# Attention and MLP in one kernel: an even pace for weight rounding, a later broadcast of inverted sums, and a direct inversion for the third pair

## The chip, the cores and the metric

The kernel runs on one core of one Trainium2 chip. The core's engines each work through their own instruction list in order: PE (TensorE, matrix products), DVE (VectorE), ACT (ScalarE), POOL (GpSimd) and SP (SyncE, which here only issues DMAs). The metric is device microseconds of one execution, as the median over several executions. "PEld" in the profile is the loading of PE's weights.

## The reference

Routed attention over 4 batches x 8 heads, 768 positions, head width 64, followed by an MLP without bias. A query attends only to keys that fall to the same of 16 centroids.

```python
q_assign = np.argmax(np.einsum('bhsd,hcd->bhsc', q_n, c_n), axis=-1)
k_assign = np.argmax(np.einsum('bhsd,hcd->bhsc', k_n, c_n), axis=-1)
mask = q_assign[:, :, :, None] == k_assign[:, :, None, :]
scores = np.where(mask, scale * np.matmul(q, k.transpose(0, 1, 3, 2)), -1000000000.0)
attn = np.exp(scores - np.max(scores, axis=-1, keepdims=True))
attn = attn / (np.sum(attn, axis=-1, keepdims=True) + 1e-09)
x = np.matmul(attn, v)      # regrouped to (3072, 512)
h = x @ w_in                # 512 x 2048
out = (h - np.tanh(h)) @ w_out
```

The two weight matrices are float64 in memory; everything else is float32.

## The kernel before

**Pairs and steps.** Two heads make a pair `n`; there are 16 pairs, four to a batch (`HP` = 4). A pair's 768 queries are handled in two halves of `TB` = 384, and the keys of a half in three steps of two 128-row tiles (`NS` = 3). The list `steps` (L850) gives 96 steps: 0 to 11 are half 0 of pairs 0 to 3, 12 to 23 their half 1, and from step 24 each pair takes six steps. The loop at L976 writes one step after another, and the order in which it writes is the order on each engine.

**One step.** `begin` (L411) computes the scores of the *following* step on PE (L419; in half 0 of pairs 1 to 3 a masking product on `hot`, L430, is added) and their exponential on ACT (L441). `value` (L466) multiplies the weights of this step with the values (L473) and, in half 0 of batch 0, also with a column of ones (L482), which gives the softmax sums. In all other halves `select` (L443) applies the mask on DVE (L451) and POOL adds up the weights (L460, L464). Two score buffers and three general PSUM buffers (`ps_f`) are shared by everything; `av` has one buffer, so `value` of a new half waits until `take` (L489, ACT) has emptied it into `xT`.

**Softmax sums.** When a half is complete (its third step, T), `total` (L494) puts the sums into a tile `den` (128 x 384, two buffers), each head's row repeated over 64 partitions. To divide, the kernel does not invert all of `den`. It writes one row per head to DRAM (`list`, L511), reads them back spread over 128 partitions (`each`, L522, step T+1), inverts 128 x 6 elements (`invert`, L528, T+2), writes them to DRAM (`back`, L530), broadcasts them back over `den` (two DMAs, L532, also T+2), and multiplies `xT` with them (`scale`, L538, T+3). The fourth pair of a batch (`last`, L517) is different: `divide` (L540) inverts `den` in place in three pieces of 128 columns (L543), multiplies (L546), and POOL keeps account of the sums and inverses (L507, L547). The list is written by this line, `i` being the step after T:

```python
for i, stage in enumerate((total, compact, invert, scale)):
```

**Weight rounding.** `w_in` and `w_out` come as 32 pieces of 512 KB in float64 words. A piece goes through: `fetch` (L185, a DMA issued by POOL into one of three `raw` buffers), `rest_of` (L195, one ACT pass, L140, into one of two `rest` buffers), `round_piece` (L200, three DVE passes, L145, L149, L152), which frees the `raw` buffer and fetches piece `at + 3`. Two pieces are rounded ahead of the loop. In the loop `paces` (L973) gives the number for each step: none in steps 0 to 2, one in steps 3 and 4, two from step 5 to step 18. On ACT, `rest_of` stands between the exponentials of the following step and `take`; on DVE, `round_piece` stands last in the step, behind `invert` and `scale`.

**What is woven in.** From step 12, batch 0's MLP products (`up` L557 with L565, then `project` L575 with L581) fill steps 12 to 47; from step 48 a Strassen form of the same for batches 1 to 3 (L755, L803), whose factors are read back from DRAM (`stream`, L681). The pieces of a pair's preparation (`turn`, `similar`, `route`, `publish`, `spread_both`, `one_hot`) are placed by `ready`. For pair 3 they are: `route` in step 4, `publish` (`q_codes`, L370) and `spread_both` (`hot`, L386) in step 5, `one_hot` (L394, L398) in step 7; step 9's scores, written in step 8, are the first to use that `hot`.

Of the kernel before, what the change touches and what calls it, by code (L numbers as in the profile page):

```python
# [30 lines left out]
F32 = mybir.dt.float32  # L31
# [7 lines left out]
P = 128  # L39
# [18 lines left out]
def kernel(  # L58
# [14 lines left out]
    B, H, S, D = q.shape  # L73
# [4 lines left out]
    HP = H // 2  # L78
# [3 lines left out]
    TB = S // 2  # L82
# [9 lines left out]
    const = ctx.enter_context(tc.tile_pool(name="const", bufs=1))  # L92
    dram = ctx.enter_context(tc.tile_pool(name="dram", bufs=6, space=DRAM))
# [7 lines left out]
    wholes = const.tile([P, TB], F32, name="wholes")  # L101
    smallest = const.tile([P, 2 * len_pieces], F32, name="smallest")
    largest = const.tile([P, 4 * (HP - 1)], F32, name="largest")
    each = const.tile([P, 2 * B * (HP - 1), 2 * TB // P], F32, name="each")
    flag = const.tile([1, 1], I32, name="flag")

    out_r = out.rearrange("(b p j) m -> b j p m", p=P, j=NCH)
# [30 lines left out]
    def low_words(dst, raw, rest):  # L138
        lo, _, rest = shaped(dst, raw, rest)
        nc.scalar.activation(out=rest, in_=lo, func=ACT.Copy, scale=2.0**-29)  # L140

    def high_words(dst, raw, rest):
        _, hi, rest = shaped(dst, raw, rest)
        bits = dst.bitcast(U32)
        nc.vector.tensor_scalar(  # L145
            out=bits, in0=hi, scalar1=3, scalar2=0x3FFFFFF8,
            op0=ALU.logical_shift_left, op1=ALU.bitwise_and,
        )
        nc.vector.scalar_tensor_tensor(  # L149
            out=bits, in0=hi, scalar=0xC0000000, in1=bits, op0=ALU.bitwise_and, op1=ALU.bitwise_or  # L150
        )
        nc.vector.tensor_tensor(out=bits, in0=bits, in1=rest, op=ALU.add)  # L152

    def fast():
# [30 lines left out]
        def fetch(at: int):  # L185
            if at >= len(PIECES):
                return
            dst, src = PIECES[at]
            if words == 1:
                nc.gpsimd.dma_start(dst, src)  # L190
                return
            raws[at] = rawp.tile([P, 2 * FQ * P], U32, name="raw")
            nc.gpsimd.dma_start(raws[at], src)

        def rest_of(at: int):  # L195
            if words == 2 and at < len(PIECES):
                rests[at] = restp.tile([P, FQ * P], U32, name="rest", tag="rest")
                low_words(PIECES[at][0], raws[at], rests[at])

        def round_piece(at: int):  # L200
            if words == 2:
                high_words(PIECES[at][0], raws.pop(at), rests.pop(at))
            fetch(at + AHEAD)
# [72 lines left out]
        pairs = [(b, p) for b in range(B) for p in range(HP)]  # L276
# [217 lines left out]
        def total(n: int, half: int):  # L494

            s = sums.pop((n, half))
            ps = s
            if not summed(n, half):
                ps = ps_f.tile([P, TB], F32, name="den", tag="f")
                for h in range(2):  # L500
                    nc.tensor.matmul(  # L501
                        ps[h * D : h * D + D], lhsT=ones, rhs=s[:, h], start=True, stop=True
                    )
            t = dens[n, half] = sump.tile([P, TB], F32, name="den")
            nc.scalar.activation(out=t, in_=ps, func=ACT.Copy, bias=EPS)
            if last(n):
                nc.gpsimd.tensor_tensor(out=wholes, in0=wholes, in1=t, op=ALU.add)  # L507
                return
            lists[n, half] = dram.tile([2, TB], F32, name="list")
            for h in range(2):  # L510
                nc.sync.dma_start(lists[n, half][h : h + 1], t[h * D : h * D + 1])  # L511
# [2 lines left out]

        lists, spots = {}, {}

        def last(n: int):  # L517
            return pairs[n][1] == HP - 1

        def compact(n: int, half: int):  # L520
            spots[n, half] = each[:, len(spots)]
# [4 lines left out]
        def invert(n: int, half: int):  # L526
            t = spots[n, half]
            nc.vector.reciprocal(out=t, in_=t)  # L528
            back = dram.tile([2, TB], F32, name="back")
            nc.sync.dma_start(back.rearrange("h n -> (h n)").rearrange("(p i) -> p i", p=P), t)  # L530
            for h in range(2):
                nc.sync.dma_start(  # L532
                    dens[n, half][h * D : h * D + D], back[h : h + 1].to_broadcast([D, TB])
                )
# [313 lines left out]
        NS = NCH // 2  # L848
        HALF = HP * NS
# [120 lines left out]
            fills[2 * (b + 1) * HALF] = (lambda b=b: strassen_items(b), 2 * HALF)  # L970


        paces = {3: 1, 4: 1}  # L973
        late, divides, makers, later = [], [], [], {}
        fill, whole, spent, since, over = [], 0.0, 0.0, 0, 1
        for at, (n, half, s) in enumerate(steps):  # L976
            b, p = pairs[n]
            following = steps[at + 1] if at + 1 < len(steps) else None
            after = steps[at + 2] if at + 2 < len(steps) else None
            if at == 4 * HALF:  # L980
                open_late()
            if at == 4 * HALF - 9:
                open_stream()
            if at in fills:
                fill, over = fills[at][0](), fills[at][1]
                whole, spent, since = sum(it[0] for it in fill), 0.0, at
            if at == 2 * HALF:
                makers = [it for i in range(2) for it in up_maker(i)]
                makers += [it for i in range(2) for it in down_maker(i)]
            now = []  # L990
            part = (at - since + 1) / over
            while fill and (spent + fill[0][0] / 2 <= whole * part or part == 1):
                now.append(fill.pop(0))
                spent += now[-1][0]
            stages = ready.get(at, {})
            if 1 in stages:
                stages[1]()
            if after and after[2] == 0 and not masked(*after[:2]):
                spread(*after[:2])
            if following and at >= NS - 1:  # L1000
                begin(following)
            share = paces.get(at, 0 if at < NS else 2)
            todays, rounding = rounding[:share], rounding[share:]
            for piece in todays:
                rest_of(piece)
            value(n, half, s)
            if s == NS - 1:
                take(n, half)
                if last(n):
                    divides = [lambda n=n, half=half, i=i: divide(n, half, i) for i in range(HCH)]  # L1010
                else:
                    for i, stage in enumerate((total, compact, invert, scale)):
                        later.setdefault(at + i, []).append(
                            lambda stage=stage, n=n, half=half: stage(n, half)
                        )

                if p == HP - 1 and (half == 1 or b == 0):
                    total(n, half)
                    late += divides
                    divides = []  # L1020
                if half == 1:
                    load(n + (HP if n < 2 else 2), (2,) if n < 2 or n >= HP else ())

            todo = []
            if following:
                todo += [lambda i=i: select(*following[:2], 2 * following[2] + i) for i in range(2)]
            todo += [stages[i] for i in (5, 3, 4, 2) if i in stages]
            todo += late + later.pop(at, [])
            late = []
            if divides:  # L1030
                todo.append(lambda n=n, half=half: total(n, half))
                late, divides = divides, []
            todo += [lambda piece=piece: round_piece(piece) for piece in todays]

            light = [i for i in range(at, 4 * HALF - 2) if i % 3 and i % 6 != 1]
            if makers and at in light:
                share = -(-len(makers) // len(light))
                todo += makers[:share]
                del makers[:share]
            if "raw" in late_pools:  # L1040
                todo += [check_done, check_done, check_on, check_on]
            slots = max(sum(it[1] for it in now), 1)
            place = iter(range(slots))
            turned_at = max(slots - 1 - now[-1][1], 0) if now else 0

            def between():
                i = next(place)
                for it in todo[i * len(todo) // slots : (i + 1) * len(todo) // slots]:
                    it()

                if i == turned_at and 0 in stages:
                    stages[0]()

            if at in fills and "raw" in late_pools:
                right_factors(b - 1)
            for it in now:
                it[2](between)
            if not now:
                between()
# [220 lines left out]
```

## Time and profile before

| what | value |
|---|---|
| median of 9 executions | 1022.82 us (1021.87 to 1027.52) |
| the profiled execution | 1024.26 us |
| its span in the profile | 1022.5 us |
| PE busy | 991.2 us (97%) |
| DVE busy | 545.3 us (53%) |
| ACT busy | 298.2 us (29%) |
| POOL busy | 491.0 us (48%) |
| mean granted PE clock | 0.994 |
| DMA traffic | 132.87 MB, mean 130 GB/s |

All times in the text are counted from the start of the profiled span unless a median is named. A row of the timeline shows start, duration, engine, line and operation, the number of instructions merged, and in brackets the idle time ahead of it with what ended it. In the chain of waits each piece is the work, the DMA or the issue that the next piece was waiting for. PE executes each float32 product in passes, so one step's eight entries at L473 are four products.

### The profile page before, as it was taken

Reading aid. Unit: us, or ns where it says so; the run is one execution under the profiler, and the core shown is the slowest. Engines: PE = TensorE matmul, PEld = TensorE weight load, DVE = VectorE, ACT = ScalarE, POOL = GpSimd, SP = SyncE. Lnnn points to the kernel's source line nnn. Section 1 sums busy time; section 2 is a strip of 40 time slices with the busy share of each in tenths; the row PEclk is TensorE's granted clock in tenths of the full one; section 3 lists DMA queues with packets and bytes.
Section 4 is the critical chain, followed back from the end, with each engine's and each line's share of the span. In section 5 each row is a group of like instructions: output and inputs, shape, how many; then the busy total and the mean of one; then the engine's idle time right before and its main releaser. Section 6 shows DMA issues by size and latency. Waiting matters only on the chain.

```text
span 1022.5 us, 16553 instructions
## 1 busy us (share of the span) xinstructions
PE 991.2 (97%) x6444; PEld 471.6 (46%) x6444; DVE 545.3 (53%) x1043; ACT 298.2 (29%) x458; POOL 491.0 (48%) x339
## 2 busy tenths in 40 slices
PE   8987999999999999999999999999999999999997
PEld 4433334334444333444455555444445555344665
DVE  6366888236665647655545456756655335544011
ACT  4444343133433333333332222333332211122000
POOL 1012443335343445676678335566779345455600
PEclk9998999999999999999999999999999999999999
DMA  8655434022736654334465455435442322333321
GB/s 211 169 149 174 132 101 123 19 72 59 199 102 166 209 165 125 116 129 124 151 196 174 143 174 155 145 117 166 145 160 76 112 102 68 109 108 112 112 94 39
DMA packets 116585, 132.87 MB, mean 130 GB/s; under 512 B 63332, under 2 KB 96276, under 8 KB 113812
## 3 DMA queue, kind: packets, MB, share of 16 engines
q1 hardware_dynamic: 110116, 110.21, 35.7%
q0 software_dynamic: 6240, 21.50, 6.3%
q8 instruction: 53, 0.87, 0.4%
q14 instruction: 32, 0.26, 0.1%
q10 hardware_dynamic: 144, 0.03, 0.0%
HBM read 110.53 MB, written 21.18 MB: 129 GB/s over the span
## 4 chain that ended last, share of the span: by engine, by line
PE 89%; DVE 4%; DMA 3%; ACT 1%; POOL 1%; issue 1%; SPq 0%; ACTq 0%; POOLq 0%; DVEq 0%
PE pd L803 20%; PE pu L755 20%; PE sc L419 13%; PE av L473 12%; PE o L581 8%; PE h L565 7%; PE sim L319 2%; PE den L501 2%; PE pt L300 2%; DMA raw<-in_moe_w_out_dram 1%; PE den L482 1%; PE warm L270 1%; ACT t L307 1%; POOL G L746 1%; PE pr L332 1%
## 5 line engine op out<-in xcount | busy, mean ns | idle before, releaser
L464 POOL TENSOR_TENSOR sum<-sum,e 128x768 f32<-128x768 f32 x112 | 205.4, 1834 | 129.4 <-DVE e L451 119.8
L451 DVE SCALAR_TENSOR_TENSOR e<-row,code,sc 128x384 f32<-128x384 bf16 x336 | 185.8, 608 | 92.7 <-ACT sc L441 87.3
L803 PE MATMUL pd<-stream,G 128*64 128x256 f32 x1728 | 192.4, 379 | 2.4 <-POOL G L746 2.4
L441 ACT ACTIVATE sc<-sc 128x768 f32<-128x768 f32 x168 | 126.0, 792 | 210.2 <-PE sc L419 209.1
L419 PE MATMUL sc<-t,t 64*128 64x384 f32 x768 | 151.8, 513 | 7.3 <-ACT e L441 7.0
L803 PEld LDWEIGHTS pd<-stream,G 128*64 128x64 f32 x1728 | 123.5, 137 | 70.5 <-issue 8.0
L473 PE MATMUL av<-e,vals 128*64 128x384 f32 x768 | 148.6, 506 | 2.0 <-ACT xT L492 0.9
L746 POOL TENSOR_TENSOR G<-G,th 128x768 f32<-128x768 f32 x48 | 86.7, 1819 | 103.7 <-ACT th L745 103.7
L755 PE MATMUL pu<-xT,stream 128*64 128x384 f32 x768 | 134.6, 487 | 0.7 <-DVE top L340 0.7
L755 PE MATMUL pu<-diff,stream 128*64 128x384 f32 x576 | 103.5, 488 | 1.9 <-DVE u L741 1.6
L419 PEld LDWEIGHTS sc<-t,t 64*128 64x128 f32 x768 | 66.3, 187 | 80.5 <-issue 38.1
L565 PE MATMUL h<-xT,w_in 128*64 128x384 f32 x512 | 86.3, 487 | 5.5 <-DVE xT L538 3.1
L473 PEld LDWEIGHTS av<-e,vals 128*64 128x64 f32 x768 | 47.5, 137 | 88.4 <-issue 84.1
L755 PEld LDWEIGHTS pu<-xT,stream 128*64 128x64 f32 x768 | 54.7, 137 | 68.4 <-issue 61.2
L581 PE MATMUL o<-w_out,g 128*64 128x512 f32 x384 | 85.7, 592 | 0.0
L460 POOL TENSOR_TENSOR sum<-e 128x768 f32<-128x768 f32 x28 | 54.8, 1957 | 60.0 <-DVE e L451 58.7
L745 ACT ACTIVATE th<-G 128x768 f32<-128x768 f32 x48 | 40.2, 843 | 122.4 <-DVE G L741 112.8
L755 PEld LDWEIGHTS pu<-diff,stream 128*64 128x64 f32 x576 | 40.6, 137 | 52.5 <-issue 44.3
L741 DVE TENSOR_TENSOR G<-pu,u 128x384 f32<-128x384 f32 x72 | 39.8, 553 | 40.6 <-PE pu L755 40.5
L565 PEld LDWEIGHTS h<-xT,w_in 128*64 128x64 f32 x512 | 36.5, 137 | 51.7 <-issue 44.5
L814 DVE TENSOR_TENSOR c<-pd,du 128x256 f32<-128x256 f32 x36 | 15.2, 422 | 69.2 <-PE pd L803 69.2
L581 PEld LDWEIGHTS o<-w_out,g 128*64 128x64 f32 x384 | 27.5, 137 | 50.6 <-issue 50.6
(121 smaller groups left out, 837.3 us busy)
## 6 DMA issues: line engine op xcount, KB each, us to landing
stream<-up_factors SPq DMA_DIRECT2D x24, 896.0 KB
stream<-down_factors SPq DMA_DIRECT2D x21, 1024.0 KB
raw<-in_moe_w_in_dram POOLq DMA_DIRECT2D x16, 512.0 KB, 5.0
raw<-in_moe_w_out_dram POOLq DMA_DIRECT2D x16, 512.0 KB, 4.5
again<-in_moe_w_in_dram SPq DMA_DIRECT2D x32, 256.0 KB
again<-in_moe_w_out_dram SPq DMA_DIRECT2D x32, 256.0 KB
x<-in_q_dram SPq DMA_DIRECT2D x32, 192.0 KB
x<-in_k_dram SPq DMA_DIRECT2D x32, 192.0 KB
```

The lines of the kernel that those rows point to most:

```text
L419: nc.tensor.matmul(sc[i][:, h, 0:TB], lhsT=turned[n, 1][r].rearrange("p a n -> p (a n)")[:, j * P : (j + 1) * P], rhs=turned[n, 0][r, half ...
L441: nc.scalar.activation(out=out, in_=sc[i][:, :, 0:TB], func=ACT.Exp, scale=SCALE)
L451: nc.vector.scalar_tensor_tensor(out=e[:, h], in0=rows[n, half][:, h], scalar=codes[n][:, 1, j // HCH, h, j % HCH : j % HCH + 1], in1=sc[: ...
L460: nc.gpsimd.tensor_tensor(out=s, in0=pair[0], in1=pair[1], op=ALU.add)
L464: nc.gpsimd.tensor_tensor(out=s, in0=s, in1=pair[i], op=ALU.add)
L473: nc.tensor.matmul(avs[n, half][h * D : h * D + D], lhsT=vals[n][:, h, j], rhs=e[i][:, h], start=(j == 0), stop=(j == NCH - 1),)
L565: nc.tensor.matmul(h[r], lhsT=w_in[i][:, c, o * P : (o + 1) * P][:, r], rhs=xT[c][:, half], start=(c == 0), stop=(c == CD - 1),)
L581: nc.tensor.matmul(acc[sub][r], lhsT=gs[f % HF][:, f // HF, sub * P : (sub + 1) * P][:, r], rhs=w_out[f // FQ][:, f % FQ], start=(f == seq ...
L745: nc.scalar.activation(out=th, in_=g[:, f], func=ACT.Tanh)
L746: nc.gpsimd.tensor_tensor(out=g[:, f].rearrange("p a n -> p (a n)"), in0=g[:, f].rearrange("p a n -> p (a n)"), in1=th.rearrange("p a n -> ...
L755: nc.tensor.matmul(ps[r], lhsT=streams[base + i][:, c, k_, r], rhs=right[c], start=(c == 0), stop=(c == CH - 1),)
L803: nc.tensor.matmul(ps[r], lhsT=left(i)[:, r], rhs=t[:, i], start=(i == 0), stop=(i == HF - 1))
```

## The change

- Sums of the third pair of batch 0 (`n == HP - 2`) are treated like those of a batch's fourth pair: `soon` takes the place of `last`, so this pair's two halves use `divide` in step T+1 and no DMA.
- For the other pairs the broadcast of the inverses is split off as `spread_out` and written in step T+3 (before: T+2), and `scale` moves to step T+5 (before: T+3).
- The pace of rounding becomes 2, 1, 2, 1, ... in steps 3 to 11, then 2, 2, 3, 3, 3, 2 and the one that is left in steps 12 to 18. Where a step has three pieces, the third `rest_of` is written behind the first `round_piece`, among the work of the step.
- `each` has two slots fewer.

```diff
-            if last(n):
+            if soon(n):
                 nc.gpsimd.tensor_tensor(out=wholes, in0=wholes, in1=t, op=ALU.add)
                 return
...
-        def last(n: int):
-            return pairs[n][1] == HP - 1
+        def soon(n: int):
+            return pairs[n][1] == HP - 1 or n == HP - 2
...
-            back = dram.tile([2, TB], F32, name="back")
+            back = lists[n, half] = dram.tile([2, TB], F32, name="back")
             nc.sync.dma_start(back.rearrange("h n -> (h n)").rearrange("(p i) -> p i", p=P), t)
+
+        def spread_out(n: int, half: int):
+            back = lists.pop((n, half))
             for h in range(2):
                 nc.sync.dma_start(
                     dens[n, half][h * D : h * D + D], back[h : h + 1].to_broadcast([D, TB])
...
-        paces = {3: 1, 4: 1}
+        paces = {at: 1 + at % 2 for at in range(NS, HALF)}
+        paces.update({at: 3 if 13 < at < 17 else 2 for at in range(HALF, HALF + 7)})
...
-            share = paces.get(at, 0 if at < NS else 2)
+            share = paces.get(at, 0)
             todays, rounding = rounding[:share], rounding[share:]
-            for piece in todays:
+            for piece in todays[:2]:
                 rest_of(piece)
...
-                    for i, stage in enumerate((total, compact, invert, scale)):
+                    for i, stage in ((0, total), (1, compact), (2, invert), (3, spread_out), (5, scale)):
...
-            todo += [lambda piece=piece: round_piece(piece) for piece in todays]
+            for i, piece in enumerate(todays):
+                todo.append(lambda piece=piece: round_piece(piece))
+                if i == 0:
+                    todo += [lambda piece=piece: rest_of(piece) for piece in todays[2:]]
```

More of the change, by code (lines that the diff above doesn't have):

```diff
@@ L103 @@
     largest = const.tile([P, 4 * (HP - 1)], F32, name="largest")
-    each = const.tile([P, 2 * B * (HP - 1), 2 * TB // P], F32, name="each")
+    each = const.tile([P, 2 * (B * (HP - 1) - 1), 2 * TB // P], F32, name="each")
     flag = const.tile([1, 1], I32, name="flag")
@@ L1008, in fast @@
                 take(n, half)
-                if last(n):
+                if soon(n):
                     divides = [lambda n=n, half=half, i=i: divide(n, half, i) for i in range(HCH)]
                 else:
-                    for i, stage in enumerate((total, compact, invert, scale)):
+                    for i, stage in ((0, total), (1, compact), (2, invert), (3, spread_out), (5, scale)):
                         later.setdefault(at + i, []).append(
```

## The prediction

> **What bounds the kernel now.** I read the engine shares first (PE 97%), then PE's busy share by slice: PE is full except at both ends and in slices 2 to 5.
>
> ```profile
> PE   8987999999999999999999999999999999999997
> ...
> PEclk9998999999999999999999999999999999999999
> ```
>
> Each digit is 25.6 us. From slice 6 (154 us) PE hardly rests: over 154 to 818 us the table by stage leaves it under 3 us idle. So only what happens before about 165 us can be gained. PE's timeline shows where:
>
> ```profile
> 62.88 1.51 PE L473 MATMUL av<-e,vals 128*64 128x384 f32 x8
> ...
> 69.44 1.63 PE L419 MATMUL sc<-t,t 64*128 64x384 f32 x8 [3.76 <-ACT e L441]
> ...
> 71.64 2.82 PE L473 MATMUL av<-e,vals 128*64 128x384 f32 x8
> ...
> 88.83 2.93 PE L419 MATMUL sc<-t,t 64*128 64x384 f32 x8 [2.97 <-ACT e L441]
> ...
> 103.56 6.67 PE L565 MATMUL h<-xT,w_in 128*64 128x384 f32 x40 [3.14 <-DVE xT L538]
> ```
>
> PE waits for exponentials, and after a gap of 3 us or more it can run at half speed (L473 2.82 us against 1.51). The first L473 of each step dates the steps: 7 at 62.88, 8 at 71.64, 9 at 78.52, 10 at 83.06, 11 at 91.69, 12 at 97.61, 13 at 112.20, 14 at 120.29, 15 at 134.16. An undisturbed step takes 4.54 us (step 6), or 4.13 without the masking product (steps 10, 11). Steps 7 to 11 so lose 4.2, 2.3, 0, 4.5 and 1.8: **12.8 us**. Step 12 takes 14.6, its products alone 10.6 (1.34 + 48 passes at 0.161 + 1.49): **4.0**. Step 14 loses a further **2.3** (PE waits at 127.6 us for g L572). Some 19 us are open in all.
>
> Why ACT is late is in the chain of waits for this window, and in the waits of DVE and ACT from 50 us on:
>
> ```profile
> 56.98 4.58 DMA q_codes<-qc
> ...
> 61.61 0.60 SPq L386
> ...
> 64.39 2.75 DMA list<-den
> ...
> 67.20 3.85 DMA each<-list
> ...
> 75.78 5.53 DMA den<-back
> ...
> 81.40 0.56 DVE xT L538
> ...
> 83.56 3.77 DMA raw<-in_moe_w_in_dram
> ...
> 88.08 0.71 ACT e L441
> ```
> ```profile
> DVE xT L538 <- DMA den<-back: 15.3, 3, 6.4
> ACT rest L140 <- DVE w_in L152: 9.7, 4, 4.2
> ```
>
> DVE reaches scale (L538) in steps 5 and 8 before the broadcast has landed, and stands still for 4.6 and 6.4 us. Behind it in order stand the roundings. They free raw buffers, so the next pieces are fetched late; ACT, in order, waits for them in L140, and behind L140 stands the exponential PE needs. The pace adds to it: from step 5 two pieces a step through three buffers. A piece's circuit is about 0.55 (L149's end to the fetch), 4.8 (median landing of a fetch), 0.7 (L140) and 1.9 (rounding), 8 us; three buffers in 1.5 steps of 4.54 give 6.8.
>
> **The change, part by part.** I walk the new order through with the durations above; the last common point is 56.9 us, where DVE ends L368.
>
> *Rounding in steps 3 to 7.* Piece 3 moves from step 4 to step 3, where DVE rests from 45.8 to 51.9 us, piece 4 to step 4; cost nothing, hidden there (1.9 us if not). Fetches run ahead: piece 6 at about 45 us (was 55.9), 7 at 55.9 (63.7), 8 at 58.6 (65.6), 9 at 60.5. Scale no longer stops DVE in step 5, so pieces 5 to 7 are done by 62.5 and ACT issues step 8's exponential at 62.9, at once. Step 7's loss goes, almost.
>
> *What is late next: step 7 on DVE.* SP still waits for q_codes (landed 61.6) before it issues `hot`; issued until 63.8, `hot` lands about 67 (4.2 and 3.7 us after the second issue for pairs 1 and 2). One-hot ends at 67.8: step 9's masking product is **0.7** late. Then scale of pair 0, whose broadcast now stands behind `hot` on SP: issued to 64.4, landed 69.7 (5.5 us). Then `invert` of pair 1: list, then each, now 1.1 us later than before through the two broadcasts ahead of them, landing about 71. DVE therefore starts rounding 8 near 71.5, having rested from 62.5. Behind that wait stand pieces 8 and 9, the fetches of 11 and 12, and ACT's `rest` of 10.
>
> *Steps 8 to 11.* `rest` of 10 waits for 8's buffer (73.4), `take` ends at 74.5, so PE's step 9 starts 74.5 instead of 72.9: **1.6** lost. Pieces 11 and 12 land at 78.0 and 79.8, the exponential for step 11 ends at 82.0, PE 0.2 late: **0.2**. The one piece of step 10 lets DVE catch up; pair 2's direct inversion costs DVE 2.6 (three L543) + 0.56 here and POOL 1.0 + 1.3, which all stands beside PE work, but pushes `select` for step 12 to 88.8: step 13's scores **1.5** late (plus 0.3 of buffer tail).
>
> *Step 12.* Before, its second MLP product waited for pair 2's scale, behind pair 3's inversion. Pair 2 is now ready in step 9, so three of four `xT` are there; only pair 3's remains. By the same arithmetic (sums 90.1, POOL L507 91.1, three L543, L546) it comes at 94.3: **1.3**. Rounding of piece 14 follows, its buffer's next fetch lands 5 us after L546, tanh and `select` free a score buffer 8 us after it while PE needs 6.5: **1.5**.
>
> *Steps 13 to 18.* Step 14's 2.3 stays: `rest` of its second piece hangs on a fetch of step 13, as before. Steps 14 to 16 get a third piece, 1.9 us of DVE each, up to 3.2 beside a POOL sum (131.31 to 134.48). DVE is busy 26.9 of 32.6 us in steps 14 to 16, so 5.7 is free, exactly 3 x 1.9; 3 x 3.2 would be 3.9 over. In the walk DVE falls 1 to 3 us behind; three `ps_f` buffers take that up until step 17, where a third product comes **0.7** late. Bounds 0 and 9.6.
>
> *After step 18* PE is full. Pair 2's second half is inverted in step 21 and needed in step 24; DVE is busy 7.1 of 25 us there: nothing (3.2 if it weren't hidden). Scale in step T+5 is read at the earliest two steps later; `total` reuses its buffer one step later, over 4.5 us. DVE's other waits for broadcasts (27.8 - 15.3 = 12.5 us) hid behind PE. SP issues broadcasts behind stream loads that wait up to 16.5 us for PE, but these are written in the same steps. I take 0 for all later batches; ends: gain 4 (all PE idle there), loss 6.4 (the longest L538 wait, once).
>
> **The sum.** Steps 7 to 12 lose 16.8 now and 0.7 + 1.6 + 0.2 + 1.8 + 1.3 + 1.5 = 7.1 then; 9.7 gained, less 0.7 in step 17, less 0.4 for clock and rounding of the walk: **8.6**. Against the profiled execution, 1024.26 (1.8 above its span): 1015.7. That execution is 1.4 above the median of the runs, so for a median I predict **1014.2**.
>
> Against the change speaks a pair of rows: q_codes took 4.58 us right behind a weight fetch (55.9 us), but 1.34 when issued at 39.4 us with no weight fetch in flight, a difference of 3.2 us. The Trainium skill, "DMA: Bandwidth & Descriptors", section "Issuing engines are not separate DMA queues", says that the queues of different engines run on the same 16 DMA engines and interleave; by it the earlier fetches of pieces 8 and 9 slow `hot` and the broadcast, and the sum would be some 3 us smaller. I keep the walk's landings, since weight fetches stood around the same DMAs before the change too, and give the 3.2 us to a rival.
>
> **The rivals.**
> - *Full recovery* (0.20). If the small DMAs take the 1.4 to 1.6 us that back<-each took at 54.3 and 150.2 us, not 3.9, and `hot` lands by 65.5, only steps 12 and 14 still wait: gain 16.8 - 2.8 = 14.0, 1008.8. For it: 69 to 74 us then holds fewer fetches. Against: SP's order is unchanged.
> - *The chain through SP still rules* (0.17). q_codes, hot, broadcast, list, each stand in one queue; if the earlier fetches make them late by the 3.2 us between the two q_codes rows, rounding 8 starts that much later: gain 8.6 - 3.2 = 5.4, 1017.4. Against: the same number of fetches, and SP has a DMA pair less ahead of q_codes.
> - *Nothing gained* (0.07). If the weights' 14 x 512 KB were limited by DMA traffic itself, pace and order would not matter. The DMA share of 0.61 from 63 to 104 us speaks against it: 1022.8.
> - *Slower: DVE overbooked in steps 14 to 16* (0.06). Three more roundings of 3.2 beside POOL's sums, and ACT's third `rest` holding each next exponential for one rounding (1.9): 9.6 + 5.7 = 15.3, less 8.6: 1029.5. It decides once DVE's lag exceeds the three `ps_f` buffers, about two products of 2.6 us; below that PE feels little. The 5.7 free us speak against it.
>
> **Numbers.** My forecast has 0.50. The range reaches past full recovery below, and above past the SP case with the later batches' loss in part: 1007 to 1020.5. About 0.2% (2 us) is what a measurement of this kernel can tell from no change; faster 0.87, same 0.07, slower 0.06.
>
> **What would show it.** Right: no DVE wait before L538 in step 5, raw fetches at 58 to 61 us, a DVE wait of several us before L394, L538 or L528 at 63 to 71 us, PE gaps under 2 us and full clock from 62 to 100 us, step 13 starting near 103. Wrong: ACT waiting over 3 us in L140 before step 9; PE gaps over 3 us in steps 14 to 17; any new PE wait after 175 us.

## The result and the profile after

The change makes the kernel faster, by less than half of what was forecast: 1019.6 us (median of 12 executions, 1018.25 to 1021.28) against 1022.82 (37 executions), ratio 0.9966 [0.9958, 0.9974]. That is 3.2 us where 8.6 were predicted. The profiled execution took 1018.24 us, its span 1016.4, at a mean granted clock of 0.997.

PE's busy share by slice and the granted clock, from the page of the changed kernel:

```profile
PE   8998899999999999999999999999999999999997
...
PEclk9999999999999999999999999999999999999999
```

Slice 2 (51 to 77 us) is full now; slice 3 went from 7 to 8 and slice 4 from 9 to 8. Steps are dated as in the prediction, by their first L473. From step 18 to the end the changed kernel takes 855.87 us, as the kernel before did (855.87): but for 0.5 us by which its step 4 starts later, all that differs lies in steps 4 to 17. PE's timeline there, with the idle time in brackets:

```profile
69.32 0.50 PE L430 MATMUL sc<-hot 64*128 64x384 bf16 x4 [1.61 <-DVE hot L398]
...
88.75 2.70 PE L419 MATMUL sc<-t,t 64*128 64x384 f32 x8 [2.63 <-DVE e L451]
91.38 2.04 PE L473 MATMUL av<-e,vals 128*64 128x384 f32 x8
...
103.70 0.92 PE L419 MATMUL sc<-t,t 64*128 64x384 f32 x4 [1.69 <-DVE e L451]
...
121.42 2.80 PE L568 MATMUL h<-xT,w_in 128*64 128x384 f32 x16 [1.47 <-DVE g L575]
...
155.52 2.80 PE L568 MATMUL h<-xT,w_in 128*64 128x384 f32 x16 [2.34 <-DVE g L575]
```

The waits for ACT's exponentials in steps 7 to 11 and the 3.14 us wait for scale in step 12 are gone. In their place stand a wait for one-hot in step 7, one for `select` in step 11, followed by half speed (L419 2.70 us against 1.56, L473 2.04 against 1.51), one of 1.69 us for `select` in step 12, and a new one in step 17. SP's issue of `hot` and DVE's timeline, one view each, show what the first is:

```profile
60.04 1.27 SPq L386 DMA_DIRECT2D hot<-q_codes  x2
```

```profile
68.62 0.42 DVE L394 TENSOR_SCALAR hot<-hot,mine_code 128x768 bf16<-128x768 bf16 x1 [5.49 <-DMA hot<-q_codes]
68.95 0.31 DVE L398 TENSOR_SCALAR hot<-hot,mine_code 128x384 bf16<-128x384 bf16 x1
69.45 0.56 DVE L541 TENSOR_TENSOR xT<-xT,den 128x384 f32<-128x384 f32 x1 [0.18 <-DMA den<-back]
```

DVE no longer stands before scale in step 5. It stands in step 7 instead, because `hot`, issued at 60.04 us, lands only at 68.6.

### The profile page after: what moved, and what is told of

It reads as the page before. It is cut to its first block, busy times and chain, and to the rows that moved or that the text cites. A ratio compares the mean times of both kernels' runs of the same rounds, so it can differ in the third digit from the quotient of the medians.

```text
span 1016.4 us, 16547 instructions
## 1 busy us (share of the span) xinstructions
PE 988.6 (97%) x6444; PEld 470.8 (46%) x6444; DVE 553.8 (54%) x1047; ACT 297.9 (29%) x458; POOL 501.3 (49%) x343
## 4 chain that ended last, share of the span: by engine, by line
PE 86%; DVE 6%; DMA 3%; ACT 2%; issue 1%; POOL 1%; SPq 0%; ACTq 0%; DVEq 0%; POOLq 0%
PE pd L806 20%; PE pu L758 20%; PE sc L419 12%; PE av L473 12%; PE o L584 8%; PE h L568 5%; DMA raw<-in_moe_w_out_dram 2%; PE sim L319 2%; PE den L501 2%; PE pt L300 2%; PE warm L270 1%; DVE w_out L149 1%; PE den L482 1%; ACT t L307 1%; POOL G L749 1%
## 5 line engine op out<-in xcount | busy, mean ns | idle before, releaser
L419 PE MATMUL sc<-t,t 64*128 64x384 f32 x768 | 151.3, 512 | 4.7 <-DVE e L451 4.3
L473 PE MATMUL av<-e,vals 128*64 128x384 f32 x768 | 146.5, 500 | 0.9 <-DVE e L451 0.9
L758 PE MATMUL pu<-diff,stream 128*64 128x384 f32 x576 | 103.5, 488 | 1.9 <-DVE u L744 1.5
L419 PEld LDWEIGHTS sc<-t,t 64*128 64x128 f32 x768 | 66.0, 186 | 78.4 <-issue 44.9
L460 POOL TENSOR_TENSOR sum<-e 128x768 f32<-128x768 f32 x28 | 57.9, 2067 | 67.5 <-DVE e L451 59.5
L473 PEld LDWEIGHTS av<-e,vals 128*64 128x64 f32 x768 | 47.1, 136 | 86.3 <-issue 82.2
```

The source lines that it names most:

```text
L419: nc.tensor.matmul(sc[i][:, h, 0:TB], lhsT=turned[n, 1][r].rearrange("p a n -> p (a n)")[:, j * P : (j + 1) * P], rhs=turned[n, 0][r, half ...
L460: nc.gpsimd.tensor_tensor(out=s, in0=pair[0], in1=pair[1], op=ALU.add)
L473: nc.tensor.matmul(avs[n, half][h * D : h * D + D], lhsT=vals[n][:, h, j], rhs=e[i][:, h], start=(j == 0), stop=(j == NCH - 1),)
L758: nc.tensor.matmul(ps[r], lhsT=streams[base + i][:, c, k_, r], rhs=right[c], start=(c == 0), stop=(c == CH - 1),)
```

## The experiments

Each ratio is against the kernel before on the same chip, with its 95% interval. "The pace" is the new `paces` with the third piece's `rest` placed later, "the later sums" are the broadcast in T+3 with scale in T+5, "direct" is the direct inversion of the third pair.

| kernel | median us | before | ratio |
|---|---|---|---|
| pace_only | 1018.84 | 1024.78 | 0.9936 [0.9914, 0.9957] |
| pace_only_2 | 1018.1 | 1024.14 | 0.9941 [0.9925, 0.9956] |
| pace_only_3 | 1018.02 | 1023.58 | 0.9942 [0.9927, 0.9956] |
| sums_later_only | 1022.08 | 1024.78 | 0.9974 [0.9960, 0.9987] |
| direct_only | 1025.87 | 1024.78 | 1.0008 [0.9996, 1.0021] |
| pace_and_sums | 1019.9 | 1024.14 | 0.9948 [0.9929, 0.9967] |
| pace_direct | 1022.06 | 1024.93 | 0.9971 [0.9958, 0.9985] |
| after_again (all three) | 1020.74 | 1024.14 | 0.9964 [0.9950, 0.9978] |
| before_round_first | 1022.48 | 1024.86 | 0.9975 [0.9964, 0.9986] |
| round_ahead | 1018.05 | 1024.14 | 0.9936 [0.9921, 0.9950] |
| spread_at_once | 1022.49 | 1024.86 | 0.9976 [0.9966, 0.9986] |
| gated | 1018.59 | 1024.93 | 0.9940 [0.9919, 0.9961] |
| gated_2 | 1017.15 | 1023.58 | 0.9932 [0.9916, 0.9948] |
| threes_apart | 1021.14 | 1024.86 | 0.9960 [0.9948, 0.9973] |
| combined | 1020.93 | 1024.86 | 0.9961 [0.9945, 0.9976] |
| pace_round_ahead | 1016.18 | 1024.93 | 0.9924 [0.9903, 0.9945] |
| pace_round_ahead_2 | 1016.39 | 1023.58 | 0.9926 [0.9906, 0.9947] |

### One part at a time

**pace_only** is the kernel before with these lines alone (and the later place of a third `rest`):

```diff
-        paces = {3: 1, 4: 1}
+        paces = {at: 1 + at % 2 for at in range(NS, HALF)}
+        paces.update({at: 3 if 13 < at < 17 else 2 for at in range(HALF, HALF + 7)})
```

> The kernel before with the new rounding pace alone (2, 1, 2, 1 in steps 3 to 11, threes in 14 to 16); sums and broadcasts as before. Theory A (DVE standing before L538 in steps 5 and 8 holds up the roundings behind it; the pace is second): those two DVE waits stay, 3 to 6 us each, and only the room from earlier fetches is gained, 1 to 3 us: 1020 to 1022. Rival B (the pace of fetches through three raw buffers is the whole cause): nearly all of the change's 3.2 us, 1019 to 1020, with the DVE waits still in the trace but harmless. Rival C (the threes cost what the rest gains): 1023 or more.

**sums_later_only** moves broadcast and scale, with `spread_out` split off as in the change; the third pair keeps its old steps, since its scale would come too late for step 12's product:

```diff
-for i, stage in enumerate((total, compact, invert, scale)):
+for i, stage in ((0, total), (1, compact), (2, invert), (2 if n == HP - 2 else 3, spread_out), (3 if n == HP - 2 else 5, scale)):
```

> The kernel before with the broadcast written one step later and scale two steps later for all pairs but the third of batch 0, which keeps its old steps (its result is needed in step 12); pace and third pair as before. Theory A: DVE no longer stands in step 5, but two pieces a step through three buffers still run late in steps 5 to 10; 2 to 4 us gained, 1019 to 1021, and the wait of PE in step 12 for the third pair's L538 stays near 3 us. Rival B: within 1 us of before, since the fetches are no faster.

**direct_only** is `soon` in the place of `last`, and nothing else:

> The kernel before with the third pair of batch 0 inverted directly, pace and steps of the other pairs as before. Theory A: the wait of PE in step 12 shrinks from 3.1 to below 2 us and SP loses three DMAs there, but 3.1 us of DVE come in step 9 among two roundings: 0 to 2 us gained, 1021 to 1023. Rival D (this part alone makes the change's gain): 1019 to 1020.

**before_again** is the kernel before, unchanged, for a second profile of it:

> The kernel before, unchanged, for a second profile. If its executions differ mainly at the start (the first profile was 1.4 us above the median), the PE gaps and half-speed products of steps 7 to 12 should be smaller here in an execution near the median: 16.8 us lost in steps 7 to 12 in the first profile, 14 to 16 expected here. If they are the same to 0.3 us, the spread lies elsewhere.

The one execution of before_again took 1027.08 us and lost 18.8 us in steps 7 to 12, not the 14 to 16 expected: the losses of one and the same kernel differ by some us between executions.

The pace alone gains 6 us of 1024, nearly twice what the whole change gains. The later sums alone gain 2.7, the direct inversion nothing. The prediction had it the other way round: scale first, the pace as something that "adds to it". Yet under the pace alone DVE still stands before scale in steps 5 and 8, for 4.6 and 6.4 us in the kernel before and little less in pace_only_2:

```profile
61.18 0.56 DVE L538 TENSOR_TENSOR xT<-xT,den 128x384 f32<-128x384 f32 x1 [4.43 <-DMA den<-back]
...
77.96 0.56 DVE L538 TENSOR_TENSOR xT<-xT,den 128x384 f32<-128x384 f32 x1 [3.57 <-DMA den<-back]
```

Why it matters less then is seen in the fetches of POOL's timeline. The kernel before, pieces 5 to 8:

```profile
43.14 0.53 POOL L193 DMA_DIRECT2D raw<-in_moe_w_in_dram  x1 [23.51 <-ACT rest L140]
55.88 0.53 POOL L193 DMA_DIRECT2D raw<-in_moe_w_in_dram  x1 [12.21 <-ACT rest L140]
63.69 0.74 POOL L193 DMA_DIRECT2D raw<-in_moe_w_in_dram  x1 [7.28 <-DVE w_in L149]
65.58 0.74 POOL L193 DMA_DIRECT2D raw<-in_moe_w_in_dram  x1 [1.15 <-DVE w_in L149]
```

The pace alone (pace_only_2), the same four pieces:

```profile
42.98 0.53 POOL L193 DMA_DIRECT2D raw<-in_moe_w_in_dram  x1 [23.92 <-ACT rest L140]
45.02 0.53 POOL L193 DMA_DIRECT2D raw<-in_moe_w_in_dram  x1 [1.51 <-DVE w_in L149]
55.72 0.53 POOL L193 DMA_DIRECT2D raw<-in_moe_w_in_dram  x1 [10.18 <-ACT rest L140]
63.35 0.74 POOL L193 DMA_DIRECT2D raw<-in_moe_w_in_dram  x1 [7.10 <-DVE w_in L149]
```

Piece 7 is the second `rest` of step 6, and ACT's exponential for step 8 stands behind it. Before, it was fetched at 63.69 us, behind DVE's stand; with one more rounding in step 3 it is fetched at 55.72, ahead of it. The stand is there, and only piece 8, not needed before step 7, waits behind it. That this fetch is what the pace gains by is read from the two traces; no run moves it alone.

### The parts in pairs

**pace_and_sums** is sums_later_only with the pace, **pace_direct** direct_only with the pace; **after_again** and **pace_only_2** are unchanged copies beside them.

> The change without the direct inversion: new pace, broadcast and scale later for all pairs but the third of batch 0, which is left at its old steps. Theory A2: PE's wait of 2.6 us for select in step 11 goes (3.1 us of DVE fewer in step 9), its wait for the third pair's L538 in step 12 comes back at 2 to 3 us; in sum within 2 us of the whole change. Rival (the direct inversion pays): 3 us or more slower than the whole change.

> The pace and the direct inversion of the third pair, without the later broadcast and scale. It completes the table of parts. If the later broadcast and scale are what takes back 2.6 us of the pace's gain, through hot, this stays at the pace's ratio of 0.994 or better, with a gap near 1.05 us in step 7 and none of the 3.14 us in step 12. If the direct inversion takes it back, through select in step 11, the ratio is that of the whole change, 0.9965, with a gap over 3 us in step 11.

> The changed kernel, unchanged, beside the others on one chip and for a second profile. Theory A2 (what differs lies in steps 4 to 18 alone; executions of one kernel scatter because PE's half-speed products after a gap come and go): the ratio to before is again near 0.9966, and the span from the start of step 18 to the end is 855.9 to 856.4 us as in every profile so far. Rival (the first comparison was off): a ratio near that of the pace alone, 0.993 to 0.994.

> The new pace alone once more, because its first ratio, 0.9936 with the interval 0.9914 to 0.9957, was better than the whole change's 0.9966 but from another chip. Theory A2 (the direct inversion of the third pair takes back what it gives): pace alone is as fast as the whole change or up to 3 us faster. Rival (chips differ): 2 to 4 us slower than the whole change on this chip.

Neither of the other parts adds to the pace: with the later sums 1.8 us are lost again on the same chip (the intervals overlap), with direct some 3 (0.9971 against 0.9941). What direct does is best seen without the pace, in PE's timeline of direct_only:

```profile
97.57 2.93 PE L419 MATMUL sc<-t,t 64*128 64x384 f32 x8 [5.52 <-DVE e L451]
```

It takes away the 3.14 us wait of step 12 (0.53 is left), but its three reciprocals (2.57 us from 84.70) stand on DVE ahead of four roundings and these ahead of `select` (96.29), all without a rest, and PE waits 5.52 us for `select` in step 11. With pace and direct the same wait is 3.32 us, in the whole change 2.63 and 2.93. The loss moved by one step.

### Why hot lands late

**spread_at_once** puts the broadcast back to T+2, so that `hot` no longer has it behind itself on SP, with scale left in T+5:

```diff
-(3, spread_out), (5, scale)
+(2, spread_out), (5, scale)
```

> The changed kernel, but with the broadcast written in step T+2 again, right behind the write of the inverses; scale stays in step T+5. Theory H (the broadcast written later, and the fetches that run ahead, share the DMA engines with the pair 3 codes, so hot lands late and PE waits 1.6 to 2.8 us in step 7; the same broadcast late in step 17 holds up the fetch of piece 30): one-hot starts about 1 us earlier, PE's gap in step 7 falls to about 1 us, step 17 falls from 16.1 to 16.3 us to about 14.8: 1.5 to 3 us faster than the change, ratio to before 0.994 to 0.995. Rival (the early fetches alone delay hot): step 7 unchanged, ratio 0.996.

PE's gap in step 7 grows to 3.1 us instead of going. What delays `hot` is seen beside pace_only_2, where SP issues q_codes and `hot` at the same times. In spread_at_once, SP's issue, POOL's fetches and DVE's one-hot, one view each:

```profile
61.15 1.26 SPq L386 DMA_DIRECT2D hot<-q_codes  x2
```
```profile
58.37 0.77 POOL L193 DMA_DIRECT2D raw<-in_moe_w_in_dram  x1 [2.11 <-DVE w_in L149]
60.28 0.53 POOL L193 DMA_DIRECT2D raw<-in_moe_w_in_dram  x1 [1.15 <-ACT e L441]
62.56 0.53 POOL L193 DMA_DIRECT2D raw<-in_moe_w_in_dram  x1 [1.75 <-DMA raw<-in_moe_w_in_dram]
```
```profile
69.44 0.42 DVE L394 TENSOR_SCALAR hot<-hot,mine_code 128x768 bf16<-128x768 bf16 x1 [6.59 <-DMA hot<-q_codes]
```

In pace_only_2 `hot` is issued at 61.06 us, but the fetches go out at 63.35, 65.24 and 67.13, and one-hot starts without a wait:

```profile
67.33 0.48 DVE L394 TENSOR_SCALAR hot<-hot,mine_code 128x768 bf16<-128x768 bf16 x1
```

With three fetches around its issue `hot` takes 8.3 us from its issue to its use, with them behind it at most 6.3. **gated** tests that on the changed kernel: one copy on POOL holds pieces 8 to 10 until `hot` has landed.

```diff
             raws[at] = rawp.tile([P, 2 * FQ * P], U32, name="raw")
+            if at == 8:
+                nc.gpsimd.tensor_copy(out=gate, in_=hots[3][:, 0, 0, 0:1])
             nc.gpsimd.dma_start(raws[at], src)
```

> The changed kernel with one small POOL copy that reads hot of pair 3, ahead of the fetch of piece 8: pieces 8, 9 and 10 are fetched only when hot has landed. If early fetches hold hot back, hot lands some 2 us earlier than in the changed kernel, DVE waits under 4 us for it (5.49 before L394 in the changed kernel's profile) and PE's gap in step 7 falls from 1.6 to 3.1 us to under 1.1; the fetches then start near 66 us, as in the kernel with the pace alone (63.4), and steps 8 to 10 may give back up to 1 us. The time comes to 1018 to 1020. If hot is late for another reason, its landing (from 61 us to 68.5 or later) and the gap stay, the fetches come late in addition, and the time rises by 1 to 3 us, to 1021 to 1024.

> The gated changed kernel, unchanged, again. If hot's landing is what the gate mends, it stays 1 to 2 us under the changed kernel's ratio of 0.9965, at 0.9945 to 0.9955, and the profile shows no PE gap over 1.2 us before step 9. If the first 1018.6 was scatter, it comes to 0.9965.

POOL's copy and DVE's one-hot in gated (the lines stand two further on there), against an issue of `hot` at 59.25 us, and PE's only idle time in steps 7 and 8, one view each:

```profile
63.50 0.39 POOL L194 CAST gate<-hot 128x1 f32<-128x1 bf16 x1 [7.72 <-DMA hot<-q_codes]
```
```profile
63.43 0.42 DVE L396 TENSOR_SCALAR hot<-hot,mine_code 128x768 bf16<-128x768 bf16 x1 [1.44 <-DMA den<-back]
```
```profile
70.78 1.62 PE L421 MATMUL sc<-t,t 64*128 64x384 f32 x8 [1.17 <-ACT e L443]
```

`hot` is used 4.2 us after its issue (5.5 in gated_2), not 8.6. Step 7 loses nothing; in step 8 the later fetches bring a gap of 1.2 us (2.7 in gated_2). The broadcast stays where the change has it, so its place on SP is not why `hot` lands late; the early fetches are. The ratios, 0.9940 and 0.9932 against the change's 0.9966 and 0.9964, say that the gate gains 2.5 to 3.5 us. The profiles do not put that on step 7 alone: steps 7 and 8 together lose 1.3 and 3.9 us in the gated kernel, 1.8 and 2.8 in the changed one, while step 11 loses 2.0 and 0.4 instead of 3.9 and 3.7. How the whole gain comes about is not shown.

### Roundings against sums on DVE

**before_round_first** tests the prediction's reason by itself. It is the kernel before with roundings ahead of `invert` and `scale` on DVE in steps 5 to 10:

```diff
-            todo += late + later.pop(at, [])
+            sums_due = late + later.pop(at, [])
+            if not NS + 2 <= at < HALF - 1:
+                todo += sums_due
...
             todo += [lambda piece=piece: round_piece(piece) for piece in todays]
+            if NS + 2 <= at < HALF - 1:
+                todo += sums_due
```

**round_ahead** does the same to the changed kernel in all steps up to 10, **pace_round_ahead** to the pace alone in steps 8 to 10; **pace_round_ahead_2** and **pace_only_3** repeat it side by side.

> The kernel before with the roundings of steps 5 to 10 ahead of total, invert and scale of the same step; pace, broadcast and third pair as before. Theory A (the roundings behind scale are the cause, as the prediction had it): no rounding waits for a broadcast any more, 3 us or more gained. Theory P (two pieces a step from step 5 ask for more than the fetch circuit gives, whatever stands ahead): 0 to 2 us gained, the ACT waits for raw pieces in steps 6 to 10 stay.

> The changed kernel with the roundings of steps 3 to 10 written ahead of total, invert, divide and scale in the same step, so that no rounding stands behind a broadcast, an inversion or a divide. Theory A2 (what is left in steps 7 to 11 is roundings behind the sums): rounding 8 starts about 1 us earlier, 11 and 12 about 3 us earlier, the gap of 2.6 us in step 11 shrinks below 1: 1.5 to 3.5 us faster than the change. Rival (what is left is the landing of hot and of the fetches): within 1 us of the change.

> The pace alone, with the sums of the kernel before, but in steps 8, 9 and 10 the roundings stand ahead of the sums on DVE. If DVE's stand before scale in step 8 (3.6 us in the pace's own profile) costs PE the 2.99 us of step 10 or the gaps around it, 1 to 2 us are gained over the pace alone: ratio 0.992. If those gaps are cover that PE doesn't feel in most executions, ratio 0.994, as the pace alone had twice.

> The pace with roundings ahead of the sums in steps 8 to 10, unchanged, again beside the pace alone and on one chip with it. If DVE's stand before scale in step 8 still costs PE something under the even pace, it is 1 to 2 us faster than the pace alone here too (some 1016 against 1018). If the first run's 1016.2 was scatter, the two agree within 0.7 us.

> The pace alone, unchanged, as the other side of that comparison: ratio 0.994 as twice before. In its profile a PE gap of 0.9 to 3 us in step 10 on ACT's exponential if the stand before scale in step 8 is felt.

Without DVE's stand in step 5 (0.72 us are left of it), but at the old pace, 2.4 us are gained: the stand does cost, and taking it away brings less than half of what the pace brings. Part of the reason is `hot` again: fetches now go out at 58.74 and 60.66 us, `hot` is issued at 61.75, and one-hot waits 2.54 us for it, where the kernel before had no such wait.

On the changed kernel roundings first bring 2.7 us on one chip (round_ahead 1018.05 against 1020.74), within the 1.5 to 3.5 expected: PE's wait for `select` in step 11 falls to 0.50 us, though the wait for one-hot in step 7 is 2.84 us there and step 17 loses 4.7. On top of the pace, roundings first in steps 8 to 10 bring 1.6 us more (1016.39 against 1018.02 on one chip, though the intervals overlap; the other repeat has the same sign). Their profiles agree with it: the gap that PE has in step 10 under the pace alone (2.99, 0.90 and 0.90 us) is in neither. This is the fastest version of all that ran.

### Step 17

**threes_apart** spreads the steps with three pieces, **combined** joins it with spread_at_once and with roundings first in steps 5 to 10:

```diff
-paces.update({at: 3 if 13 < at < 17 else 2 for at in range(HALF, HALF + 7)})
+paces.update({at: 2 + at % 2 for at in range(HALF, HALF + 7)})
```

> The changed kernel with steps 12 to 18 paced 2, 3, 2, 3, 2, 3 and the rest of one, so that no two steps of three follow each other. Theory T (three steps of three in a row put DVE and the raw buffers behind, and step 17 pays): step 17 falls from 16.2 us by 1 to 2.5 us, with no more than 0.5 us lost in steps 13 to 16: 1 to 2 us faster than the change. Rival (the late broadcast in step 17 does it): step 17 stays above 15.5 us, within 0.7 us of the change.

> The changed kernel with three edits: roundings of steps 5 to 10 ahead of the sums, broadcast again in step T+2, threes apart. If the three act where the profiles put them (step 7: 1 us, step 11: 2.5 us, step 17: 2 us), it is 4 to 6 us faster than the change, ratio to before 0.991 to 0.993, and faster than the pace alone (0.994). If one gap only gives way to the next, it is no better than the pace alone.

Step 17 loses nothing then, but step 14, with a third piece in step 13, loses 7.7 us instead of 1.5. PE's timeline of threes_apart:

```profile
121.39 0.87 PE L501 MATMUL den<-sum,ones 128*64 128x384 f32 x4 [1.44 <-DVE g L575]
125.52 5.39 PE L568 MATMUL h<-xT,w_in 128*64 128x384 f32 x16 [3.26 <-DVE g L575]
```

Neither version differs measurably from the changed kernel. The chain of waits of the changed kernel says what holds step 17:

```profile
147.47 5.91 DMA raw<-in_moe_w_out_dram
...
153.46 0.10 ACT rest L140
...
154.49 0.40 ACT th L573
...
154.91 0.57 DVE g L575
...
155.52 2.80 PE h L568 x16
```

A fetch of `w_out` lands after 5.91 us; ACT's `rest` for it stands ahead of the tanh that frees PE's buffer. In the six profiles with the pace's three pieces and the old sums, step 17 loses 1.1 to 1.9 us, in the seven with the later scale 2.3 to 4.7. The waits alone are 1.0 to 1.8 us against 2.2 to 3.0; the rest is half speed behind them. In pace_only_2 the same fetch landed after 4.76 us; here the broadcast, issued at 146.87 us, is in flight beside it. But that is not the whole of it: in spread_at_once the broadcast is issued at 143.89 us and the fetch lands after 4.85, and step 17 loses 4.5 all the same (there PE waits 2.86 us at L300 for ACT's copy, L307, and not for g).

## Why the prediction was right and where it was wrong

The direction, the place (all before step 18) and the range held; the size did not: 3.2 us came of 8.6. The steps that failed are three terms of the walk and the reading of the median. Step 11's `select` cost 2.0 us more than reckoned, step 17 1.8 more, and `hot` in step 7 1.4 more because its landing was kept as it had been. The walk's terms, against what the two profiles of the changed kernel lose over undisturbed steps:

| step | predicted | measured |
|---|---|---|
| 7, hot | 0.7 | 1.8, 2.3 |
| 8, `rest` of 10 | 1.6 | 0, 0.4 |
| 10 | 0.2 | 0.3, 0.7 |
| 11, select | 1.5 + 0.3 | 3.9, 3.7 |
| 12 | 1.3 + 1.5 | 2.6, 3.6 |
| 14 | 2.3 | 1.5, 1.6 |
| 17 | 0.7 | 2.4, 2.6 |

By the means of the two, 3.6 us more are lost than the walk had.

- **"I keep the walk's landings" (step 7).** This failed, and what the row that was set aside pointed at, DMAs of SP slowed by the fetches, was the thing to follow. The row itself, q_codes at 4.58 against 1.34 us, holds more than a fetch: in the kernel before the broadcast pair (L532, 55.75 us) also stood right ahead of it. In the two profiles of the changed kernel, with a fetch about 1 us ahead of it but no broadcast, q_codes took 2.51 and 3.15 us; so the 3.2 us were not the fetch's alone. Fetches did stand around the same DMAs before, but *behind* `hot`, held there by the very DVE wait that the change removes. The Trainium skill, "DMA: Bandwidth & Descriptors", section "Issuing engines are not separate DMA queues", says that transfers started by different engines share the 16 DMA engines and interleave; the two kernels with `hot` at 61.1 us (8.3 against at most 6.3 us) and the gate (4.2 and 5.5 against 8.6) agree with it. The rival built on this had 1017.4.
- **"pushes `select` for step 12 to 88.8" (step 11).** The mechanism was right, the term too small: gaps of 2.63 and 2.93 us instead of 1.8 in all, and half speed after them. So the direct inversion, reckoned as a gain in step 12, gives nothing by itself. With the roundings ahead of the inversion (round_ahead) step 11 loses 1.1.
- **Step 17's 0.7.** Sized with DVE's load alone, it came to 2.5: what the walk lacked is the fetch behind the second of three roundings, whose `rest` stands on ACT ahead of the tanh. With the pace alone that costs 1.1 to 1.6; why it is more with the later sums is not settled.
- **"Scale no longer stops DVE in step 5 ... Step 7's loss goes, almost".** True as far as it goes (4.2 became 2.1), but not the main cause: the pace alone takes step 7's loss to 1.2 to 1.5 with the stand in place.
- **Step 8** was costed at 1.6 and lost next to nothing; step 12 came out within 0.5 by its mean, step 14 0.8 better than reckoned. The 0 for all later batches held (855.87 and 855.70 us from step 18 on, 855.87 and 855.90 before).
- **"That execution is 1.4 above the median of the runs, so for a median I predict 1014.2".** This carries the 1.4 over as if it lay outside the steps that the change mends. The excess of the execution that the losses were read from was in those steps, as far as two profiles can tell: the second one of the kernel before lost 3.4 us more in steps 4 to 17 than the first (121.47 against 118.08) and the same from step 18 on. The 3.6 of the walk and this 1.4 make 5.0 of the 5.4 us between forecast and result.

Of the signs listed, no wait before L538 in step 5, fetches at 58 to 61 us and a DVE wait before L394 came true; "PE gaps under 2 us and full clock from 62 to 100 us" did not (2.63 in step 11, then half speed), and step 13 started at 104.5 us, not near 103.

What stays open: why step 17 is worse with the later sums, by what way the gate gains, and how much of the 1.6 us of pace_round_ahead is real.

## What to carry to other kernels

A wait can be a gate that nobody planned: before taking it away, list what starts earlier then, and look for a transfer on the critical path that would now share the DMA engines with it. Where one wait holds up a queue of prefetches, try first to move the prefetch that is needed next ahead of the wait; that was cheaper here, and brought more, than removing the wait. And measure the parts of a change one by one: here one part was worth nearly twice the whole.

## What the runs showed of the hardware

The same gap on PE, 3.14 us before the same 40 passes of step 12, is followed by different speeds. In the kernel before they took 6.67 us; in its second profile and in pace_only:

```profile
103.78 8.32 PE L565 MATMUL h<-xT,w_in 128*64 128x384 f32 x40 [3.14 <-DVE xT L538]
```
```profile
97.35 9.66 PE L565 MATMUL h<-xT,w_in 128*64 128x384 f32 x40 [3.14 <-DVE xT L538]
```

The granted clock in the profile says the same: 0.50 from 97.3 to 102.0 us in pace_only, 1.00 from 103.5 to 110.2 in the kernel before. A gap near 3 us so costs up to 3 us more or nothing, and the program does not decide which: the pace alone, one kernel, took 9.66, 8.37 and 6.67 us for these passes in its three profiles. It happened after shorter gaps too: in before_again 16 passes at L565 took 4.47 us behind a gap of 2.11 us, in pace_round_ahead the same 16 passes took 2.80 behind one of 2.41. The Trainium skill, "TensorE: Matmul & The Clock Gate", section "What's actually happening", puts the drop to half speed at an idle window of about 3.4 us that runs freely; the scatter here fits a free-running window, the length does not, since shorter gaps already brought half speed. For a prediction this means that a term for such a gap has two ends, and that a loss read from one profile holds a few us of scatter.
